# One scaled pair product per head instead of seven levels, in a kernel that runs a decayed recurrence and then a multiplicative feed-forward block

## The chip, the cores and the metric

The kernel runs on one core of one Trainium2 chip. The number that counts is the device time of one execution in microseconds (us). An engine works through its own instructions in order and waits on semaphores for the others: PE (TensorE, matmul; PEld is its weight load), DVE (VectorE), ACT (ScalarE), POOL (GpSimd), and SP, which here issues all the transfers.

## The reference

```python
r, k, v: (4, 8, 768, 48)   w, u: (8, 48)
for t in range(S):                                 # S = 768
    kt, vt, rt = k[:, :, t], v[:, :, t], r[:, :, t]
    cur = einsum('bhd,bhe->bhde', u[None] * kt, vt)
    y[:, :, t] = einsum('bhd,bhde->bhe', rt, state + cur)
    state = w[None, :, :, None] * state + einsum('bhd,bhe->bhde', kt, vt)
x = y.transpose(0, 2, 1, 3).reshape(B * S, H * D)  # (3072, 384)
a, b = x @ w1, x @ w2                              # (3072, 1024)
out = (a * b @ w3) @ w_out                         # (3072, 384)
```

`w` lies between 0.85 and 0.95. The four feed-forward weights arrive as float64, that is as 64-bit words; the kernel rounds them to float32 on the chip. All else is float32.

## The kernel before

**Tiling.** The sequence is cut into six chunks of 128 tokens. A *unit* is one chunk of one of the four batches, so there are 24 units, in the order chunk by chunk and, within a chunk, batch by batch. Two heads form a pair: head dimension 48 is padded to 64, so that a pair fills 128 partitions.

**The first part, per unit.** `load` fetches k, r and v. `turn` (L211) transposes k and r on PE, and ACT copies them out. The matrix A[t, s] of a chunk is built in seven *levels* (`scale` L219, `level` L236): level l joins pairs of tokens whose places differ by a block of 2^l, so that only powers of w with an exponent of at least 0 occur. Every level needs its own scaled operands, KL (POOL, L229) and RL (DVE, L232; for level 0 ACT and POOL, L223 and L224), its own matmuls (L241, L262, L256), and its own copy into A: for levels 0 to 4 a predicated copy with a mask on DVE (L242, L244, L263), for levels 5 and 6 a copy on ACT (L258). `output` (L268) multiplies A and the state with v and r (L276, L279), ACT copies the result, and ten small transfers put it into x with the layout that the second part wants. `update` (L294) brings the state forward (POOL L299 and L306, PE L302, DVE L308).

**The weights.** `weight` (L150) converts one piece of up to 128 x 512 numbers from 64 bits: three products on POOL (L161, L170, L171), four instructions on DVE (L162, L165, L166, L168), one on ACT (L169). There are 36 pieces. `fold` (L185) transposes w3 and multiplies it with w_out, so that the second part needs only w34 = w3 w_out.

**The second part, per chunk.** `ab` (L326), eight times: six matmuls 128 x 512 for a and b (L331, L336), a copy on ACT, a product on DVE (L337). `o` (L339), four times: eight matmuls 128 x 384 with w34 (L342), a copy on ACT, a transfer out.

**What sets the order.** The loop at the end (L360 to L380) interleaves by hand: beside the units of chunk 0 run w_out and w3, beside those of chunk 1 w1 and w2, beside chunk c from 2 on the second part of chunk c - 2; the second part of chunks 4 and 5 stands behind all units. The framework then orders each engine's queue by priority and dependences; an engine executes its queue strictly in that order. PSUM is split into four banks for the levels, two for the rest of the first part and two for the second part.

Of the kernel before, what the change touches and what calls it, by code (L numbers as in the profile page):

```python
# [8 lines left out]
F32 = mybir.dt.float32  # L9
# [3 lines left out]
ALU = mybir.AluOpType  # L13


@with_exitstack
def kernel(
# [25 lines left out]
    The second part uses (a b w3) w_out = (a b) (w3 w_out), with w3 w_out made  # L43
    once on chip.
    """
# [3 lines left out]
    C = 128  # L49
    NCH = S // C  # L50
# [7 lines left out]
    LEVELS = 7  # L58

    const = ctx.enter_context(tc.tile_pool(name="const", bufs=1))  # L60
    work = ctx.enter_context(tc.tile_pool(name="work", bufs=2))
    psA = ctx.enter_context(tc.tile_pool(name="psA", bufs=4, space=bass.MemoryType.PSUM))
    psM = ctx.enter_context(tc.tile_pool(name="psM", bufs=2, space=bass.MemoryType.PSUM))
    psF = ctx.enter_context(tc.tile_pool(name="psF", bufs=2, space=bass.MemoryType.PSUM))

# [1 line left out]
    ident = const.tile([P, P], F32)  # L67
    make_identity(nc, ident)
    masks = []
    for l in range(LEVELS):  # L70
        L = 1 << l
        n = C // (2 * L)
        m = const.tile([P, n], F32, name=f"mask{l}")
        nc.gpsimd.memset(m, 1.0)
        nc.gpsimd.affine_select(out=m, in_=m, compare_op=ALU.is_ge, fill=0.0, base=0,
                                pattern=[[-2 * L, n]], channel_multiplier=1)
        nc.gpsimd.affine_select(out=m, in_=m, compare_op=ALU.is_ge, fill=0.0, base=L - 1,
                                pattern=[[2 * L, n]], channel_multiplier=-1)
        masks.append(m)

# [1 line left out]
    NIN = 3  # L82
    knat, rnat, vnat = ([const.tile([C, H, PAD], F32, name=f"{nm}nat{i}") for i in range(NIN)] for nm in "krv")
    for t in knat + rnat + vnat:
        nc.vector.memset(t[:, :, D:PAD], 0.0)
    AT = [const.tile([P, NP, 2, C], F32, name=f"AT{i}") for i in range(2)]
    for t in AT:
        nc.vector.memset(t, 0.0)
    KL = [None] + [const.tile([P, NP, C], F32, name=f"KL{l}") for l in range(1, LEVELS)]
    RL = [const.tile([P, NP, 2, C // 2 + C], F32, name="RL0")]  # L90
    RL += [const.tile([P, NP, 2, C // 2], F32, name=f"RL{l}") for l in range(1, LEVELS)]
    for t in RL + KL[1:]:
        nc.gpsimd.memset(t, 0.0)
    st = [const.tile([P, NP, 2, PAD], F32, name=f"st{b}") for b in range(B)]
    for t in st:
        nc.gpsimd.memset(t, 0.0)

# [1 line left out]
    units = [(c, b) for c in range(NCH) for b in range(B)]  # L99

    def load(n):
        if n >= len(units):
            return
        c, b = units[n]
        ts = slice(c * C, (c + 1) * C)
        nc.sync.dma_start(out=knat[n % NIN][:, :, :D], in_=k[b, :, ts, :].rearrange("h t d -> t h d"))
        nc.sync.dma_start(out=rnat[n % NIN][:, :, :D], in_=r[b, :, ts, :].rearrange("h t d -> t h d"))
        nc.sync.dma_start(out=vnat[n % NIN][:, :, :D], in_=v[b, :, ts, :].rearrange("h t d -> t h d"))

    wu = const.tile([2 * NP, 2, PAD], F32)  # L110
    nc.vector.memset(wu, 0.0)
    nc.sync.dma_start(out=wu[0:NP, :, :D], in_=w.rearrange("(p i) d -> p i d", i=2))
    nc.sync.dma_start(out=wu[NP:2 * NP, :, :D], in_=u.rearrange("(p i) d -> p i d", i=2))
    load(0)
    load(1)

# [5 lines left out]
    ps = psM.tile([P, 2 * NP], F32, tag="m", name="ps_wu")  # L122
    nc.tensor.transpose(ps, wu.rearrange("a i d -> a (i d)"), ident[0:2 * NP, 0:2 * NP])
    wucol = const.tile([P, 2 * NP, 1], F32)
    nc.vector.tensor_copy(out=wucol.rearrange("x a o -> x (a o)"), in_=ps)
    ucol = wucol[:, NP:2 * NP, :]
    pw = const.tile([P, NP, C], F32)
    pr = const.tile([P, NP, C], F32)
    wn = const.tile([P, LEVELS, NP, 1], F32)
    nc.vector.memset(pw[:, :, 0:1], 1.0)  # L130
    nc.vector.memset(pr[:, :, C - 1:C], 1.0)
    cur = wucol[:, 0:NP, :]
    for l in range(LEVELS):
        n = 1 << l
        by = cur.to_broadcast([P, NP, n])
        nc.vector.tensor_mul(pw[:, :, n:2 * n], pw[:, :, 0:n], by)
        nc.vector.tensor_mul(pr[:, :, C - 2 * n:C - n], pr[:, :, C - n:C], by)
        nc.vector.tensor_mul(wn[:, l], cur, cur)
        cur = wn[:, l]
    wc = cur  # L140
    ps = psM.tile([P, NP, C], F32, tag="m", name="ps_pr")
    for p in range(NP):
        nc.tensor.transpose(ps[:, p, :], pr[:, p, :], ident)
    prn = const.tile([C, H, PAD], F32)
    nc.vector.tensor_copy(out=prn.rearrange("t h d -> t (h d)"), in_=ps.rearrange("x p t -> x (p t)"))

# [1 line left out]
    PIECE = 512  # L148

    def weight(dst, src):  # L150
        """dst: [P, n] float32 on chip; src: the same [P, n] of a weight."""
        if src.dtype != U64:
            nc.sync.dma_start(out=dst, in_=src)
            return
        n = src.shape[1]
        raw = work.tile([P, PIECE], U64, tag="raw", bufs=2, name="raw")[:, :n]
        nc.sync.dma_start(out=raw, in_=src)
        lo, hi = (raw.bitcast(U32).rearrange("p (n z) -> p n z", z=2)[:, :, z] for z in range(2))
        high, bits, low = (work.tile([P, PIECE], F32, tag="tmp", bufs=6, name=nm)[:, :n] for nm in ("high", "bits", "low"))
        # Magnitudes under 2^-126 become zero. The high word read as float32 is ordered as the magnitudes are.  # L160
        nc.gpsimd.tensor_mul(bits, hi.bitcast(F32), hi.bitcast(F32))  # L161
        nc.vector.scalar_tensor_tensor(high, bits, (1.125 * 2.0 ** -15) ** 2, hi.bitcast(F32), ALU.is_ge, ALU.mult)  # L162
        # Sign and top exponent bit stay; the other exponent bits and the upper 20 of the fraction move up by 3.
        hb, bb = high.bitcast(U32), bits.bitcast(U32)
        nc.vector.tensor_scalar(bb, hb, 0x07FFFFFF, 3, ALU.bitwise_and, ALU.logical_shift_left)  # L165
        nc.vector.scalar_tensor_tensor(hb, hb, 0xC0000000, bb, ALU.bitwise_and, ALU.bitwise_or)  # L166
        # The lower 32 bits of the fraction, at the power of two that the number has.
        nc.vector.tensor_scalar(bb, hb, 0xFF800000, None, ALU.bitwise_and)  # L168
# [4 lines left out]
    def ab_weight(q, z):  # L173
        for dst, src in ((w1, moe_w1), (w2, moe_w2)):
            js = slice(z * PIECE, (z + 1) * PIECE)
            weight(dst[:, q, js], src[q * P:(q + 1) * P, js])

# [1 line left out]
    wo = {}  # L179

    def out_weight(c):
        wo[c] = work.tile([P, DM], F32, tag="abt", bufs=KF + 4, name=f"wo{c}")
        weight(wo[c], moe_w_out[c * P:(c + 1) * P, :])

    def fold(j):  # L185
        w3n = work.tile([P, DF], F32, tag="w3", bufs=3, name=f"w3n{j}")
        for z in range(DF // PIECE):
            js = slice(z * PIECE, (z + 1) * PIECE)
            weight(w3n[:, js], moe_w3[j * P:(j + 1) * P, js])
        w3T = work.tile([P, KF, P], F32, tag="w3", bufs=3, name=f"w3T{j}")  # L190
        for i in range(2):
# [11 lines left out]
    def rows(i):  # L203
        return slice(i * PAD, (i + 1) * PAD)
# [89 lines left out]
    def update(n):  # L294
        c, b = units[n]
        if c == NCH - 1:
            return
# [113 lines left out]
```

## Time and profile before

| | us |
|---|---|
| device time, median of 3 runs (892.48 to 893.22) | 892.74 |
| span of the profiled execution, first to last instruction | 888.0 |
| busy in it: PE / DVE / POOL / ACT | 784.0 / 504.3 / 387.7 / 166.2 |
| instructions on PE / DVE / POOL / ACT | 3589 / 845 / 400 / 325 |
| conversions of weights | 36 pieces |

For the profiled execution only the span is given; the median lies 4.7 us over it, and that is taken as what lies around the span. A float32 matmul appears in the profile as two PE instructions, a transpose as one. Busy shares are averages over two stretches with different limits, so they have to be read by stage: chunks 0 and 1 end at about 300 us, and from there on PE is the engine that the others wait for.

### The profile page before, as it was taken

What the parts mean: (1) busy time and instruction counts of PE and PEld (TensorE: products, weight loads), DVE (VectorE), ACT (ScalarE), POOL (GpSimd) and SP (SyncE); (2) the same over time, 40 slices, a digit from 0 to 9 for tenths busy, and PEclk for the clock granted to TensorE, in tenths of its full rate; (3) what the DMA queues carried; (4) which work ended last, traced back from release to release, by engine and by line L of the source; (5) the groups of instructions that cost most, each with busy time, mean ns of one, the idle gap of its engine ahead of it and who ended that gap; (6) DMA issues with size and microseconds to landing.
All of it is one profiled execution on the core that took longest, in us unless ns stands there. A gap on an engine that the chain in (4) does not pass through costs nothing.

```text
span 888.0 us, 10047 instructions
## 1 busy us (share of the span) xinstructions
PE 784.0 (88%) x3589; PEld 481.9 (54%) x3589; DVE 504.3 (57%) x845; ACT 166.2 (19%) x325; POOL 387.7 (44%) x400
## 2 busy tenths in 40 slices
PE   4566687567787899999999999999999999999998
PEld 2454355345555555666565666556665556445444
DVE  6999988679999964654365436644554442010010
ACT  1122223231121221112112111211111211110110
POOL 8678787787778852343234323333332220000000
PEclk9787688877998999999999999999999999999999
DMA  7134224213233110032001131110310001000000
GB/s 133 46 76 114 95 96 131 86 56 107 60 92 84 28 27 18 14 68 54 18 10 27 26 73 28 27 28 17 74 28 10 0 12 43 18 0 27 9 0 36
DMA packets 96649, 42.08 MB, mean 47 GB/s; under 512 B 79704, under 2 KB 91992, under 8 KB 96600
## 3 DMA queue, kind: packets, MB, share of 16 engines
q1 hardware_dynamic: 96600, 41.45, 18.7%
q8 instruction: 29, 0.48, 0.2%
q14 instruction: 20, 0.16, 0.1%
HBM read 31.98 MB, written 4.72 MB: 41 GB/s over the span
## 4 chain that ended last, share of the span: by engine, by line
PE 66%; DVE 23%; POOL 7%; issue 3%; ACT 0%; DMA 0%; SPq 0%; POOLq 0%; ACTq 0%; DVEq 0%
PE ps_a L331 14%; PE ps_o L342 14%; PE ps_b L336 13%; DVE RL L232 7%; PE ps_a L262 7%; PE ps_d L241 5%; PE ps_a L256 4%; DVE high L162 4%; PE ps_y L276 3%; DVE AT L263 3%; PE ps_y L279 3%; DVE high L166 2%; DVE bits L165 2%; POOL low L170 2%; DVE bits L168 2%
## 5 line engine op out<-in xcount | busy, mean ns | idle before, releaser
L232 DVE TENSOR_TENSOR RL<-rT,pw 64x256 f32<-64x256 f32 x288 | 195.7, 681 | 27.8 <-PE ps_a L256 22.0
L229 POOL TENSOR_TENSOR KL<-kT,pr 128x256 f32<-128x256 f32 x144 | 116.3, 817 | 166.1 <-PE ps_a L256 98.4
L337 DVE TENSOR_TENSOR abt<-ps_b,a 128x512 f32<-128x512 f32 x48 | 33.2, 692 | 196.6 <-PE ps_b L336 196.5
L331 PE MATMUL ps_a<-xT,w 128*128 128x512 f32 x288 | 136.9, 602 | 0.0
L336 PE MATMUL ps_b<-xT,w 128*128 128x512 f32 x288 | 133.0, 596 | 0.8 <-DVE abt L337 0.8
L342 PE MATMUL ps_o<-w,abt 128*128 128x384 f32 x384 | 128.8, 489 | 0.0
L262 PE MATMUL ps_a<-RL,KL 128*128 128x128 f32 x768 | 105.0, 297 | 24.5 <-DVE AT L244 24.5
L262 PEld LDWEIGHTS ps_a<-RL,KL 128*128 128x128 f32 x768 | 103.4, 212 | 38.7 <-issue 22.6
L342 PEld LDWEIGHTS ps_o<-w,abt 128*128 128x128 f32 x384 | 71.4, 190 | 46.4 <-issue 1.3
L241 PE MATMUL ps_d<-RL,kT 128*128 128x384 f32 x192 | 79.2, 545 | 19.2 <-DVE AT L263 17.6
L336 PEld LDWEIGHTS ps_b<-xT,w 128*128 128x128 f32 x288 | 54.9, 191 | 69.2 <-issue 67.5
L263 DVE COPY_PREDICATED AT<-mask,ps_a 128x512 f32<-128x512 int32 x96 | 81.7, 851 | 17.2 <-PE ps_a L262 14.1
L256 PE MATMUL ps_a<-RL,KL 128*32 128x64 f32 (+1 forms) x576 | 58.0, 246 | 25.9 <-ACT AT L258 20.0
L331 PEld LDWEIGHTS ps_a<-xT,w 128*128 128x128 f32 x288 | 51.0, 190 | 48.2 <-issue 45.6
L256 PEld LDWEIGHTS ps_a<-RL,KL 128*32 128x32 f32 (+1 forms) x576 | 44.4, 122 | 58.4 <-ACT AT L258 36.3
L258 ACT COPY AT<-ps_a 32x256 f32<-32x256 f32 (+1 forms) x72 | 30.5, 433 | 222.5 <-DVE AT L263 167.6
L242 DVE COPY_PREDICATED AT<-ident,ps_d 128x256 f32<-128x256 int32 x96 | 42.3, 459 | 47.2 <-PE ps_d L241 46.9
L170 POOL TENSOR_TENSOR low<-low,bits 128x512 f32<-128x512 f32 (+1 forms) x36 | 47.5, 1322 | 36.3 <-DVE bits L168 35.1
L273 POOL TENSOR_TENSOR rw<-rT,pw 128x512 f32<-128x512 f32 x20 | 25.9, 1297 | 85.3 <-ACT rT L217 85.3
L224 POOL TENSOR_TENSOR RL<-rT,wucol 64x512 f32<-64x512 f32 x48 | 53.3, 1111 | 14.3 <-PE ps_d L241 8.3
L241 PEld LDWEIGHTS ps_d<-RL,kT 128*128 128x128 f32 x192 | 36.1, 206 | 40.6 <-DVE AT L263 11.3
L333 ACT COPY a<-ps_a 128x512 f32<-128x512 f32 x48 | 28.1, 585 | 137.9 <-PE ps_a L331 136.9
(66 smaller groups left out, 773.8 us busy)
## 6 DMA issues: line engine op xcount, KB each, us to landing
raw<-in_moe_w_dram SPq DMA_DIRECT2D x28, 512.0 KB, 3.5
knat<-in_k_dram SPq DMA_DIRECT2D x24, 192.0 KB, 3.2
rnat<-in_r_dram SPq DMA_DIRECT2D x24, 192.0 KB, 3.8
vnat<-in_v_dram SPq DMA_DIRECT2D x24, 192.0 KB, 2.8
out_dram<-osb SPq DMA_DIRECT2D x24, 192.0 KB, 2.2
xT<-y SPq DMA_DIRECT2D x144, 24.0 KB, 1.8
raw<-in_moe_w_out_dram SPq DMA_DIRECT2D x8, 384.0 KB, 3.3
xT<-y SPq DMA_DIRECT2D x48, 16.0 KB, 1.8
```

What stands on the lines that cost most here:

```text
L170: nc.gpsimd.tensor_mul(low, low, bits)
L224: nc.gpsimd.tensor_mul(RL[0][rows(i), :, i, C // 2:], rT[n][rows(i)], ucol[rows(i)].to_broadcast([PAD, NP, C]))
L229: nc.gpsimd.tensor_mul(halves(KL[l], L)[:, :, :, 0, :], halves(kT[n], L)[:, :, :, 0, :], pr[:, :, None, C - L:C].to_broadcast([P, NP, m, L]))
L232: nc.vector.tensor_mul(RL[l][rows(i), :, i, :].rearrange("x p (n a) -> x p n a", a=L), halves(rT[n], L)[rows(i), :, :, 1, :], pw[rows(i), ...
L241: nc.tensor.matmul(ps, lhsT=kT[n][:, p, :], rhs=RL[0][:, p], start=True, stop=True)
L242: nc.vector.copy_predicated(at[:, p], ident.bitcast(I32)[:, None, :].to_broadcast([P, 2, C]), ps[:, :, C // 2:])
L256: nc.tensor.matmul(ps[s0:s0 + L, p, :, g * L:(g + 1) * L], lhsT=KL[l][:, p, s0:s0 + L], rhs=RL[l][:, p, :, g * L:(g + 1) * L], start=True, ...
L262: nc.tensor.matmul(ps[:, p], lhsT=KL[l][:, p, :], rhs=RL[l][:, p], start=True, stop=True)
L263: nc.vector.copy_predicated(at.rearrange("s p i (n z a) -> s (p i) n z a", z=2, a=L)[:, :, :, 1, :], masks[l].bitcast(I32)[:, None, :, Non ...
L331: nc.tensor.matmul(pa, lhsT=w1[:, q, js], rhs=xT[c][:, q, :], start=(q == 0), stop=(q == KM - 1))
L336: nc.tensor.matmul(pb, lhsT=w2[:, q, js], rhs=xT[c][:, q, :], start=(q == 0), stop=(q == KM - 1))
L342: nc.tensor.matmul(po, lhsT=abt[j][:, b * C:(b + 1) * C], rhs=w34[:, j, :], start=(j == 0), stop=(j == KF - 1))
```

## The change

The seven levels go. With w within [0.6, 1.6], k is multiplied by w^(63 - s) and r by w^(t - 64) for the places s and t in the chunk (`scale`, on DVE, before the transposes), and one product per head gives w^(t - 1 - s). The powers (`up`, `down`) are made once, with a reciprocal. `pairs` multiplies the two heads of a pair on their own 64 rows each, into two PSUM tiles, and two predicated copies per unit keep t > s. The diagonal is computed apart: a product of k, r and u on DVE with a sum over d, written by eight scaled copies of the identity on ACT. The state is kept in scaled form, so that r and k need no further scaling in `output` and `update`; the factor w^128 is applied in `update` on DVE. x gets a permuted order of its 384 columns, so that ACT copies three quarters of a unit's output straight into x and six transfers of 16 partitions carry the rest; the rows of w1 and w2 are fetched in the same order, four transfers a piece instead of one. The conversion leaves POOL: six instructions on DVE and one on ACT. The loop's neighbours are reordered: beside chunk 0 half of w1 and w2, beside chunk 1 the other half and the second part's products a b of chunk 0, beside chunk 2 those of chunk 1, w_out and three eighths of w3, and so on; the second part lags by one chunk, its output product somewhat more.

All of that is one arm of a branch. A flag, computed on DVE from the smallest and the largest w, is read by every engine into a register; where w lies outside, the other arm runs with the seven levels, built with small POOL instructions. Both arms are in the program.

```diff
+    inside = nc.values_load(flag[0:1, 0:1], min_val=0, max_val=1, ...
...
-        nc.gpsimd.tensor_mul(bits, hi.bitcast(F32), hi.bitcast(F32))
-        nc.vector.scalar_tensor_tensor(high, bits, (1.125 * 2.0 ** -15) ** 2, hi.bitcast(F32), ALU.is_ge, ALU.mult)
...
-        nc.scalar.mul(low, lo, 2.0 ** -52)
-        nc.gpsimd.tensor_mul(low, low, bits)
-        nc.gpsimd.tensor_add(dst, high, low)
+            nc.scalar.activation(out=power, in_=hi.bitcast(F32), func=ABS)
+            nc.vector.scalar_tensor_tensor(dst, power, 1.125 * 2.0 ** -15, hi.bitcast(F32), ALU.is_ge, ALU.mult)
+            nc.vector.tensor_scalar(tb, hb, 0x07FFFFFF, 3, ALU.bitwise_and, ALU.logical_shift_left)
+            nc.vector.scalar_tensor_tensor(hb, hb, 0xC0000000, tb, ALU.bitwise_and, ALU.bitwise_or)
+            nc.vector.tensor_scalar(pb, hb, 0xFF800000, None, ALU.bitwise_and)
+            nc.vector.scalar_tensor_tensor(t, lo, 2.0 ** -52, power, ALU.mult, ALU.mult)
+            nc.vector.tensor_add(dst, dst, t)
...
+        def scale(n):
+            kn, rn = kin[n % NIN], rin[n % NIN]
+            if fast:
+                nc.vector.tensor_mul(ks[n % NS][:, :, :D], kn, pn["k"][:, :, :D])
+                nc.vector.tensor_mul(rs[n % NS][:, :, :D], rn, pn["r"][:, :, :D])
...
+            nc.vector.tensor_mul(ruk, kn, rn)
+            nc.vector.tensor_mul(ruk, ruk, ub)
+            nc.vector.tensor_reduce(dg, ruk, AX.X, ALU.add)
...
+                    nc.scalar.activation(out=AT[n][:, i, p, :], in_=ident, func=COPY, scale=dg[:, h:h + 1])
...
+        def pairs(n):
+            if fast:
+                ps = [psA.tile([C, NP, C], F32, tag="a", name=f"ps_a{n}_{i}") for i in range(2)]
+                for p in range(NP):
+                    for i in range(2):
+                        nc.tensor.matmul(ps[i][:, p, :], lhsT=kT[n][rows(i), p, :], rhs=rT[n][rows(i), p, :],
+                                         start=True, stop=True)
+                for i in range(2):
+                    nc.vector.copy_predicated(AT[n][:, i], later.bitcast(I32)[:, None, :].to_broadcast([C, NP, C]), ps[i])
+                return
...
+            nc.scalar.copy(out=y, in_=ps[:, NP - 1, :])
+            nc.scalar.copy(out=xT[c][:, :, bs], in_=ps[:, 0:KM, :])
+            for i in range(2):
+                for q in range(KM):
+                    at = i * PAD + q * HOLE
+                    nc.sync.dma_start(out=xT[c][i * PAD + D:(i + 1) * PAD, q, bs], in_=y[at:at + HOLE, :])
...
+                if c:
+                    nc.vector.tensor_add(old, new, old)
+                    nc.vector.tensor_mul(old, old, by)
...
+        beside = [
+            W12[0],
+            merge(W12[1], AB(0, range(KH))) + AB(0, range(KH, KF)),
+            merge(AB(1), WO + W3(range(3))),
+            merge(AB(2, range(KH)), W3(range(3, KF))) + O(0) + AB(2, range(KH, KF)),
+            merge(O(1) + O(2), AB(3)),
+            merge(O(3), AB(4)),
+        ]
+        tail = O(4) + AB(5) + O(5)
...
+    with tc.If(inside > 0) as chosen:
+        program(True)
...
+    with chosen.Else():
+        program(False)
```

On PE, a unit in chunk 2 of the kernel before (products of the levels 3 to 6 of a unit, then its output and state products, with the last a and b of the second part between):

```order
L262 MATMUL ps_a_3_2357<-RL_134,KL_127 128x128 x4
L262 MATMUL ps_a_4_2366<-RL_135,KL_128 128x128 x4
L256 MATMUL ps_a_5_2375<-RL_136,KL_129 32x2x32 x4
L331 MATMUL ps_a_7_2390<-xT_394,w_169 128x512 x2
L256 MATMUL ps_a_5_2375<-RL_136,KL_129 32x2x32 x4
L331 MATMUL ps_a_7_2390<-xT_394,w_169 128x512
L336 MATMUL ps_b_7_2396<-xT_394,w_170 128x512 x3
L256 MATMUL ps_a_6_2401<-RL_137,KL_130 64x128 x4
L276 MATMUL ps_y_2410<-rw_2411,st_153 128x128
L302 MATMUL ps_s_2439<-vnat_110,ks_2437 128x128 x3
L279 MATMUL ps_y_2410<-AT_121,vnat_110 64x128 x2
```

And on PE of the changed kernel, the end of one unit of chunk 2 and the begin of the next one's products (kT and rT are the transposes, ps_y the output, ps_s the state, ps_a and ps_b with w the second part, w3T a fold, and ps_a with kT the product of a head):

```order
L310 MATMUL ps_kT_1583<-ident,ks_75 128x128 x4
L310 MATMUL ps_rT_1590<-ident,rs_77 128x128 x4
L365 MATMUL ps_y_1608<-rT_1430,st_85 128x128 x4
L369 MATMUL ps_y_1608<-AT_1364,vnat_74 64x128 x8
L392 MATMUL ps_s_1640<-vnat_74,ks_76 128x128 x4
L416 MATMUL ps_a_7_1648<-xT_681,w_93 128x512 x3
L421 MATMUL ps_b_7_1654<-xT_681,w_94 128x512 x3
L276 MATMUL ps_w3T_0_1660<-ident,w3n_1597 128x128 x4
L321 MATMUL ps_a_0_1712<-rT_1595,kT_1588 128x128
L321 MATMUL ps_a_1_1713<-rT_1595,kT_1588 128x128
```

The last two rows come four times per unit, and they are all that is left of the levels; the folds of w3 now stand among the second part's products.

On DVE of the changed kernel, the last conversion of w1 and w2 (w_94 is w2, raw its 64-bit piece), with the next unit's scaling and diagonal woven in and the second part's products behind it:

```order
L245 SCALAR_TENSOR_TENSOR w_94<-power,raw_81 128x512
L290 TENSOR_TENSOR ks_76<-kin_66,pnk 128x8x48
L247 TENSOR_SCALAR t<-w_94 128x512
L248 SCALAR_TENSOR_TENSOR w_94<-w_94,t 128x512
L291 TENSOR_TENSOR rs_78<-rin_69,pnr 128x8x48
L250 TENSOR_SCALAR power<-w_94 128x512
L297 TENSOR_TENSOR ruk_1074<-kin_66,rin_69 128x384
L251 SCALAR_TENSOR_TENSOR t<-raw_81,power 128x512
L298 TENSOR_TENSOR ruk_1074<-ruk_1074,ub 128x384
L252 TENSOR_TENSOR w_94<-w_94,t 128x512
L299 TENSOR_REDUCE dg_1075<-ruk_1074 128x8
L422 TENSOR_TENSOR abt_4_966<-ps_b_4_973,a_4_971 128x512
```

In the kernel before, the DVE rows between the four instructions of a conversion were those of the levels, and the first product abt (L337) came only in chunk 2, behind all conversions. Now the product abt_4 of chunk 0 stands right behind the last conversion of w2, because it needs it.

On DVE before, the corresponding place, the last conversions and the first product of the second part:

```order
L166 SCALAR_TENSOR_TENSOR high<-high,bits 128x512
L165 TENSOR_SCALAR bits<-high 128x512
L168 TENSOR_SCALAR bits<-high 128x512
L166 SCALAR_TENSOR_TENSOR high<-high,bits 128x512
L242 COPY_PREDICATED AT_121<-ident,ps_d_0_1968 128x256
L168 TENSOR_SCALAR bits<-high 128x512
L244 COPY_PREDICATED AT_121<-mask_75,ps_d_0_1968 128x128
L242 COPY_PREDICATED AT_121<-ident,ps_d_1_1972 128x256
```

Behind these rows stand five more masked copies of level 0, the scaled operands and the copies of levels 1 and 2, and then abt_0.

More of the change, by code (lines that the diff above doesn't have):

```diff
@@ L82 @@
[L82 to L91, printed above, removed]
@@ L140 @@
[L140 to L168, printed above, removed]
-        nc.scalar.mul(low, lo, 2.0 ** -52)
-        nc.gpsimd.tensor_mul(low, low, bits)
-        nc.gpsimd.tensor_add(dst, high, low)
@@ L203, in rows @@
-    def rows(i):
-        return slice(i * PAD, (i + 1) * PAD)
-    def halves(t, L):
-        return t.rearrange("x p (n z a) -> x p n z a", z=2, a=L)
-    kT, rT, xT = {}, {}, {}
-    def turn(n):
-        for dst, src, nm in ((kT, knat, "kT"), (rT, rnat, "rT")):
-            ps = psM.tile([P, NP, C], F32, tag="m", name=f"ps_{nm}{n}")
-            for p in range(NP):
-                nc.tensor.transpose(ps[:, p, :], src[n % NIN][:, 2 * p:2 * p + 2, :].rearrange("t h d -> t (h d)"), ident)
-            dst[n] = work.tile([P, NP, C], F32, tag=nm, name=f"{nm}{n}")
-            nc.scalar.copy(out=dst[n], in_=ps)
@@ L310, in attention @@
-    def attention(n):
-        def step(l):
-            level(n, l)
-            if n + 1 < len(units):
-                scale(n + 1, l)
-        steps = [lambda: turn(n + 1)] if n + 1 < len(units) else []
-        steps += [lambda l=l: step(l) for l in range(LEVELS)]
-        return steps + [lambda: output(n), lambda: update(n)]
-    def ffn(c):
-        steps = []
+    landed[1] = fetch(ab_pieces[1])
+    ends = const.tile([1, 3], F32)
+    flag = const.tile([1, 1], I32)
+    nc.vector.tensor_reduce(ends[:, 0:1], wrow, AX.X, ALU.min)
@@ L378, with AB, O, first @@
-    for c in range(NCH - LAG, NCH):
-        for step in ffn(c):
-            step()
+        def AB(c, js=range(KF)):
+            return [lambda c=c, j=j: ab(c, j) for j in js]
+        def O(c):
+            return [lambda c=c, b=b: o(c, b) for b in range(B)]
+        def first(i):
+            if i not in landed:
+                landed[i] = fetch(ab_pieces[i])
+            convert(ab_pieces[i], landed[i])
+        half = len(ab_pieces) // 2
+        W12 = [[lambda i=i: first(i) for i in range(z * half, (z + 1) * half)] for z in range(2)]
```

465 lines of the change are left out of this document (283 added, 182 removed).

## The prediction

> **What bounds the kernel now.** I read the page's busy times and chain first, then busy times by stage.
>
> ```profile
> span 888.0 us, 10047 instructions
> PE 784.0 (88%) x3589; PEld 481.9 (54%) x3589; DVE 504.3 (57%) x845; ACT 166.2 (19%) x325; POOL 387.7 (44%) x400
> PEclk9787688877998999999999999999999999999999
> PE 66%; DVE 23%; POOL 7%; issue 3%; ACT 0%; DMA 0%; SPq 0%; POOLq 0%; ACTq 0%; DVEq 0%
> ```
>
> ```profile
> core 0: us, PE busy (x) PEld busy (x) DVE busy (x) ACT busy (x) POOL busy (x), PEclk, DMA share, GB/s
> 0.00:25.00 25.00, 8.90 (x29) 5.66 (x29) 16.77 (x47) 6.21 (x11) 21.30 (x55) 0.93 0.69 118
> 25.00:300.00 275.00, 194.42 (x1003) 135.19 (x1004) 246.13 (x351) 61.62 (x119) 212.04 (x184) 0.81 0.30 85
> 300.00:748.00 448.00, 444.06 (x2181) 272.75 (x2180) 230.31 (x433) 83.03 (x167) 154.31 (x162) 1.00 0.14 30
> 748.00:888.00 140.00, 136.67 (x379) 68.27 (x377) 11.07 (x16) 15.31 (x28) 0.00 (x0) 1.00 0.05 16
> ```
>
> There are two kernels in one. Up to 300 us (chunks 0 and 1, and all conversions) DVE is busy 246.1 of 275 us, 89.5%, with POOL close behind, and PE has gaps and a granted clock of 0.81. From 300 us on PE is busy 444.1 of 448 us at a clock of 1.00. So the front is priced by DVE and the rest by PE.
>
> What PE takes for each kind of work at full clock is read from where the next row starts:
>
> ```profile
> 639.97 0.44 PE L279 MATMUL ps_y<-AT,vnat 128*64 128x128 f32 x4
> 640.34 0.49 PE L276 MATMUL ps_y<-rw,st 128*128 128x128 f32 x2
> 640.76 0.44 PE L279 MATMUL ps_y<-AT,vnat 128*64 128x128 f32 x4
> ...
> 643.03 5.33 PE L342 MATMUL ps_o<-w,abt 128*128 128x384 f32 x16
> 648.19 0.60 PE L215 MATMUL ps_kT<-ident,knat 128*128 128x128 f32 x4
> 648.63 0.60 PE L215 MATMUL ps_rT<-ident,rnat 128*128 128x128 f32 x4
> 649.06 2.75 PE L241 MATMUL ps_d<-RL,kT 128*128 128x384 f32 x8
> 651.65 1.95 PE L262 MATMUL ps_a<-RL,KL 128*128 128x128 f32 x16
> 653.43 2.74 PE L331 MATMUL ps_a<-xT,w 128*128 128x512 f32 x6
> 656.01 2.74 PE L336 MATMUL ps_b<-xT,w 128*128 128x512 f32 x6
> ```
>
> A float32 matmul is two instructions. Hence one 128x512 takes 2.58/3 = 0.86 us, one 128x384 5.16/8 = 0.645, one 128x128 1.78/8 = 0.223, a transpose 0.44/4 = 0.109, and one of the half-array matmuls of L279 0.37/2 = 0.185. Going from L276's full array to halves costs 0.42 - 0.22 = 0.20 us.
>
> DVE's price depends on POOL:
>
> ```profile
> 121.38 1.74 DVE L162 SCALAR_TENSOR_TENSOR high<-bits,raw 128x512 f32<-128x512 f32 x1 [0.93 <-POOL bits L161]
> 123.37 1.16 DVE L165 TENSOR_SCALAR bits<-high 128x512 uint32<-128x512 uint32 x1
> ...
> 125.90 0.68 DVE L162 SCALAR_TENSOR_TENSOR high<-bits,raw 128x512 f32<-128x512 f32 x1
> 126.50 0.41 DVE L168 TENSOR_SCALAR bits<-high 128x512 uint32<-128x512 uint32 x1
> ```
>
> ```profile
> 162.54 0.60 DVE high L166
> 163.14 0.34 DVE bits L165
> 163.48 0.34 DVE bits L168
> 163.81 0.61 DVE high L166
> 169.36 0.61 DVE AT L263
> 170.34 1.37 issue
> ```
>
> The same L162 takes 1.74 us in one place and 0.68 in the other; the long one runs beside POOL's products. In the chain, where only the step to the next instruction counts, 512 elements cost 0.61 us and a one-source instruction 0.34.
>
> ```profile
> L229 POOL TENSOR_TENSOR KL<-kT,pr 128x256 f32<-128x256 f32 x144 | 116.3, 817 | 166.1 <-PE ps_a L256 98.4 <-PE ps_a L262 66.0
> L337 DVE TENSOR_TENSOR abt<-ps_b,a 128x512 f32<-128x512 f32 x48 | 33.2, 692 | 196.6 <-PE ps_b L336 196.5
> L308 DVE TENSOR_TENSOR st<-ps_s,st 64x256 f32<-64x256 f32 x40 | 16.8, 420 | 41.0 <-POOL st L306 40.7
> L217 ACT COPY kT<-ps_kT 128x512 f32<-128x512 f32 x24 | 14.1, 586 | 37.7 <-PE ps_kT L215 37.6
> L258 ACT COPY AT<-ps_a 32x256 f32<-32x256 f32 x48 | 17.4, 362 | 185.6 <-DVE AT L263 167.6 <-PE ps_a L256 18.0
> ```
>
> From L308 to L337, 256 more elements cost 272 ns, so 384 elements cost 0.61 - 0.14 = 0.48 us on DVE (0.27 for one source).
>
> **The change part by part.** *PE.* A unit loses the products of levels 0 to 4 (2.59 + 2 x 1.78 = 6.2 us) and two more levels, and gains eight products on half the rows. Their price is not in the trace. The nearest row is L279, half the columns: 0.185 us. Below lies 0.112 (both halves at once), above 0.42 (L276 with its switch at every one). I take 0.185 and one switch of 0.20 per unit into them and one into the output. PE then has 288 matmuls 128x512 (247.4 us), 192 of 128x384 (123.8), eight folds of eight transposes and eight 128x384 (48.3), 192 transposes (20.9), 192 products and 192 output halves (71), 160 state matmuls 128x128 (35.8), some 48 switches (9.6), 1 for the tables: **558 us** instead of the 784.0 busy now.
>
> *DVE and POOL.* POOL falls silent after the tables, so DVE runs at the short prices. A conversion is then four instructions of 0.61 and two of 0.34: 3.1 us on DVE, and it can no longer overlap with POOL's three. A unit costs five instructions of 0.48 (scaling, diagonal, sum), two masked copies and two for the state at 0.61: 4.8 us, in place of the levels' operands and copies. The tensor_reduce and the read of the 32-bit low words have no row; between 0.42 (L308) and 1.74 (L162 beside POOL) I take the short price, since nothing of POOL is beside them. All of DVE is about 249 us, so DVE sets only the front.
>
> *The front, by the queues.* The last thing on which PE must wait for a conversion is b_4 of chunk 0: it needs the last piece of w2. Ahead of that piece's last instruction DVE has 12 conversions (37.4), 49 instructions of 0.48 (23.5), 18 masked copies (11.0), 14 for the state (8.5), four products abt (2.4) and 22 small ones of the tables (3.7): 86.5 us. At the 89.5% of before that is 96.7 us. Behind this point PE still has, of the same list, 254 x 0.86 + 123.8 + 48.3 + 112 x 0.109 + 236 x 0.185 + 104 x 0.223 + 30 x 0.20 = **475.7 us**. Queued on PE behind b_4 are the last products of chunk 0 and all of chunk 1's, and DVE's abt_4 stands right behind the conversion that releases it, so nothing else is late there. The later checkpoints are looser: at the masked copy of unit 12, DVE has had 162 us and PE has 367 to go.
>
> *The start.* DVE can begin when w has come and the branch is taken.
>
> ```profile
> 5.37 2.31 DMA wu<-in_u_dram
> ```
>
> In before, w and u are there at 7.7 us; I take 8.0 until the flag is made. No branch is in the trace. It costs nothing at least; for the most I take four times the longest "issue" gap, 4 x 1.37 = 5.5; I take two, 2.7, one to read the flag and one at the end. Start: 10.7 us.
>
> *Sum against the profiled execution.* 10.7 + 96.7 + 475.7 = 583.1. Behind the last matmul:
>
> ```profile
> 884.70 0.48 ACT L345 COPY osb<-ps_o 128x384 f32<-128x384 f32 x1 [4.68 <-PE ps_o L342]
> ```
>
> 888.0 - 884.7 = 3.3 us for copy, transfer and end. PE idled 3.9 of 448 us in its stretch: 4 more. Between the conversions of the first half of w1 and w2 and the last of w2, PE has 37 us of work at full clock; at a clock of 0.81 that is 46, DVE has (86.5 - 51)/0.895 = 40: 6 more. Span 596.4; the median lies 4.7 over the span: 601, taken as **602 us**.
>
> *Hidden.* ACT gains 192 scaled copies of 128 elements (between 0.26, by the line through L217 and L258's 256, and 0.59, L217; 50 to 113 us) and the conversions' first step, and has about 180 us in 600; DVE and PE wait for it only in the front. SP gets 36 more weight transfers and 96 fewer of x; the DMA share is 0.30 at most behind the start. If that cover goes, it is in the front, and the second rival prices it.
>
> On the halves the Trainium skill's page "TensorEngine Tiling (Array Packing)", section Theoretical Speedup, gives up to twofold for a contraction of 64 rows or less; the row L279 shows 0.223 to 0.185, a gain of a sixth. By that rule the 116 products left behind the checkpoint would take 8.5 us less. Its section Key Properties says that a change of mode drains the array, which speaks against mixing halves with full matmuls; the 0.20 us agrees. On the branch, the page "Runtime: NRT & Kernel Launch", Instruction fetch mechanics, says that a taken branch breaks the prefetch and stalls; no run here shows it.
>
> **The rivals.**
> 1. *The front overlaps fully* (the table says why it could: no POOL beside DVE, which was the second engine of the old front). DVE at 100%: 86.5 for 96.7, no clock loss, products at 0.112: 602 - 10 - 6 - 8 = 578.
> 2. *The front becomes a chain of waits.* Each unit goes DVE, PE, ACT, PE, DVE, PE with two buffers, and DVE's and PE's loads up to unit 12 are nearly alike (162 and 182 us), so each waits for the other. For it: the clock of 0.81 where PE was not full. At 70% DVE takes 124 us, 27 more, and chunk 2's 105 us of PE at 85% 18 more: 647. The Trainium skill's page "TensorE: Matmul & The Clock Gate", Part 1, has the clock halved after an idle window; the 0.81 is what such halves average to here.
> 3. *The other arm runs,* or the change doesn't do what it says: the flag comes out 0. Then per unit and level POOL makes 12 small products. Each is priced from L229: a quarter of its 0.82 at least. 24 x 7 x 12 = 2016 of them give 413 to 1650 us on POOL alone, with memsets and masks on top and nothing of the old double buffering; at half of L229 already 824 us, and with a front and second part of about 300 behind, **over 1,100, slower**. It decides at a w under 0.6 or over 1.6; the reference has 0.85 to 0.95.
>
> **How the numbers follow.** Forecast (590 to 625) 0.58; rival 1 (under 590) 0.15; rival 2 (625 to 665) 0.20; later still, but under 890, 0.05; rival 3 0.02. The range takes rival 1's 578 and its bound without any branch (2.7 less), and rival 2's 647 and the half products' upper price in part (116 x 0.23 = 27 on the forecast): **575 to 650**. A change within 0.2% is about what a measurement of this kernel cannot tell from none; so faster 0.97, same 0.01, slower 0.02.
>
> **What would show it.** In the changed profile POOL busy under 30 us and DVE about 250; L245 and its fellows near 0.69 and 0.41, not 1.7; PE busy near 550, full at clock 1.00 from about 120 us on; the half products starting 0.09 us apart. The prediction is wrong if PE shows gaps behind chunk 2, if the masked copies or the reduce are dear, or if the halves cost more than full products.

## The result, and the profile after

The changed kernel takes 607.11 us (median of 4 runs, 606.07 to 614.0) against 892.98 us (4 runs, 892.48 to 893.66): a ratio of 0.682, interval 0.678 to 0.685. The forecast was 602, in a range of 575 to 650.

The page of the changed kernel: span, busy time of each engine, then PE's busy share and clock in forty slices, and the chain's shares.

```profile
span 604.2 us, 6718 instructions
PE 554.2 (92%) x2441; PEld 321.0 (53%) x2441; DVE 261.5 (43%) x497; ACT 172.6 (29%) x423; POOL 10.3 (2%) x36
...
PE   0298987679999999999999999999999999999996
PEclk9999999699999999999999999999999999999999
...
PE 86%; DVE 5%; SPq 4%; DMA 2%; ACT 1%; issue 1%; DVEq 0%; ACTq 0%
```

The fast arm ran: POOL has 36 instructions. PE's 784.0 us of work are 554.2 now, DVE's 504.3 are 261.5. The weak place is the sixth to ninth slice, about 75 to 136 us. The same by stages, with busy time of each engine, granted clock and DMA share:

```profile
core 0: us, PE busy (x) PEld busy (x) DVE busy (x) ACT busy (x) POOL busy (x), PEclk, DMA share, GB/s
0.00:30.00 30.00, 4.35 (x19) 3.56 (x20) 18.25 (x55) 9.47 (x24) 10.27 (x36) 1.00 0.68 134
30.00:133.00 103.00, 85.02 (x549) 55.03 (x548) 73.86 (x133) 41.18 (x107) 0.00 (x0) 0.95 0.49 100
133.00:599.00 466.00, 464.51 (x1876) 262.43 (x1874) 169.40 (x311) 121.43 (x292) 0.00 (x0) 1.00 0.20 52
```

Behind 133 us PE is busy 464.5 of 466 us. In the front, from 30 to 133 us, *no* engine is full: DVE is busy 73.9 of 103 us (72%), PE 85.0. An engine that alone set the pace would be full there, so the front waits for something else, or for a chain between the engines. The chain of waits names one thing, in two pieces of the front (start, duration, what):

```profile
46.67 0.51 SPq L380
...
49.75 0.59 SPq L380
...
50.44 0.53 SPq L99
51.01 3.69 DMA rin<-in_r_dram
54.72 0.57 DVE rs L291
...
66.63 0.42 SPq L133
...
67.15 0.52 SPq L380
...
70.24 0.59 SPq L380
...
70.94 2.71 DMA raw<-in_moe_w_dram
73.66 0.69 DVE w L245
...
131.96 0.62 DVE w L252
...
132.62 1.99 PE ps_b L421 x4
```

SP issues all transfers in one order. The six transfers that carry a unit's x (L380) take about 0.6 us each to issue, and behind them stands first the load of the next k and r (L99 and L100), then the next piece of a weight. DVE waits for both. From 30 to 133 us eight units' x transfers hold SP's queue for 3.7 to 4.4 us each, 31 us in all. SP's own waits in the same window (us in total, times, longest):

```profile
SPq L133 <- DVE t L251: 28.1, 6, 7.8
SPq L380 <- ACT AT L304: 4.7, 1, 4.7
...
SPq L380 <- ACT xT L376: 0.4, 1, 0.4
```

So in the front SP stands still at L380 for only 5 us; what L380 costs there is the time of issuing. (SP waits far longer at L380 behind 133 us, where PE is full all the same.) The 28.1 us are waits for a buffer of raw words that DVE has to read first. PE's granted clock was also 0.50 for 10.2 us of the front (the last three numbers of the row are clock, DMA share and GB/s):

```profile
108.30:118.50 10.20, 6.53 (x21) 3.87 (x21) 5.60 (x11) 4.76 (x12) 0.00 (x0) 0.50 0.79 137
```

The last two rows of the chain are the checkpoint of the prediction, the conversion that releases b_4 of chunk 0: PE goes on at 132.6 us.

### The profile page after: what moved, and what is told of

Same layout as the page of the kernel before. It is cut to its first block, busy times and chain, and to the rows that moved or that the text cites. A ratio compares the mean times of both kernels' runs of the same rounds, so it can differ in the third digit from the quotient of the medians.

```text
span 604.2 us, 6718 instructions
## 1 busy us (share of the span) xinstructions
PE 554.2 (92%) x2441; PEld 321.0 (53%) x2441; DVE 261.5 (43%) x497; ACT 172.6 (29%) x423; POOL 10.3 (2%) x36
## 4 chain that ended last, share of the span: by engine, by line
PE 86%; DVE 5%; SPq 4%; DMA 2%; ACT 1%; issue 1%; DVEq 0%; ACTq 0%
PE ps_o L427 21%; PE ps_a L416 20%; PE ps_b L421 20%; PE ps_w L280 7%; PE ps_y L369 4%; PE ps_a L321 4%; PE ps_y L365 3%; PE ps_s L392 3%; PE ps_rT L310 2%; PE ps_kT L310 2%; DMA rin<-in_r_dram 1%; SPq L380 1%; PE ps_w3T L276 1%; SPq L133 1%; DMA raw<-in_moe_w_dram 1%
## 5 line engine op out<-in xcount | busy, mean ns | idle before, releaser
L304 ACT ACTIVATE AT<-ident,dg 128x128 f32<-128x128 f32 x192 | 58.9, 394 | 6.8 <-DVE dg L299 6.8
L280 PE MATMUL ps_w<-wo,w3T 128*128 128x384 f32 x128 | 43.0, 489 | 0.6 <-ACT w3T L277 0.5
L324 DVE COPY_PREDICATED AT<-later,ps_a 128x512 f32<-128x512 int32 x48 | 32.3, 721 | 18.8 <-PE ps_a L321 17.9
L321 PEld LDWEIGHTS ps_a<-rT,kT 64*128 64x128 f32 x384 | 25.3, 195 | 16.5 <-issue 8.4
L321 PE MATMUL ps_a<-rT,kT 64*128 64x128 f32 x384 | 31.4, 298 | 2.8 <-ACT rT L312 2.8
L280 PEld LDWEIGHTS ps_w<-wo,w3T 128*128 128x128 f32 x128 | 23.7, 190 | 16.0 <-ACT w3T L277 1.0
L244 ACT ACTIVATE power<-raw 128x512 f32<-128x512 f32 (+1 forms) x36 | 23.4, 653 | 25.2 <-DVE t L251 19.4
L369 PE MATMUL ps_y<-AT,vnat 128*64 128x128 f32 x384 | 28.8, 280 | 0.9 <-ACT kT L312 0.6
L392 PE MATMUL ps_s<-vnat,ks 128*128 128x128 f32 x160 | 24.3, 286 | 0.0
L369 PEld LDWEIGHTS ps_y<-AT,vnat 128*64 128x64 f32 x384 | 21.6, 136 | 4.9 <-ACT kT L312 0.8
L251 DVE SCALAR_TENSOR_TENSOR t<-raw,power 128x512 f32<-128x512 uint32 (+1 forms) x36 | 23.6, 656 | 0.3
L299 DVE TENSOR_REDUCE dg<-ruk 128x8 f32<-128x384 f32 x24 | 13.1, 547 | 24.3 <-ACT AT L304 24.2
```

Source lines behind the costliest of these rows:

```text
L280: nc.tensor.matmul(ps, lhsT=w3T[:, kc, :], rhs=wo[kc], start=(kc == 0), stop=(kc == KF - 1))
L304: nc.scalar.activation(out=AT[n][:, i, p, :], in_=ident, func=COPY, scale=dg[:, h:h + 1])
L321: nc.tensor.matmul(ps[i][:, p, :], lhsT=kT[n][rows(i), p, :], rhs=rT[n][rows(i), p, :], start=True, stop=True)
L324: nc.vector.copy_predicated(AT[n][:, i], later.bitcast(I32)[:, None, :].to_broadcast([C, NP, C]), ps[i])
L369: nc.tensor.matmul(ps[rows(i), p], lhsT=vnat[n % NV][:, 2 * p + i, :], rhs=AT[n][:, i, p, :], start=not c, stop=True, skip_group_check=True)
L392: nc.tensor.matmul(ps[:, p], lhsT=kk[:, 2 * p:2 * p + 2, :].rearrange("t h d -> t (h d)"), rhs=vnat[n % NV][:, 2 * p:2 * p + 2, :], start= ...
```

## The experiments

Each ratio is to the kernel before, measured on the same chip. The changed kernel was not run again beside the experiments, so differences to its 607.11 us carry the spread of its own four runs (606.07 to 614.0).

**1 and 2. The x transfers on another queue.** Theory: SP's order makes the front late.

```diff
-                    nc.sync.dma_start(out=xT[c][i * PAD + D:(i + 1) * PAD, q, bs], in_=y[at:at + HOLE, :])
+                    nc.gpsimd.dma_start(out=xT[c][i * PAD + D:(i + 1) * PAD, q, bs], in_=y[at:at + HOLE, :])
```

and the same with `nc.scalar`.

> The six small transfers of a unit's x are issued by POOL's queue, which is idle, instead of SP's. In the changed kernel PE reached the third matmul of b_4 of chunk 0 at 132.6 us, 19 us later than the prediction's working had it. Theory Q (SP's queue): the loads and the weight pieces stand behind those transfers on SP, 3.7 us of issue per unit and a wait for ACT's copy; freed of them, b_4 comes 8 to 15 us earlier and the time falls to 592 to 600. Rival C (a chain of waits between DVE, PE and ACT with two buffers): SP is not what is waited for; b_4 stays within 3 us and the time at 604 to 610.

> The same six transfers issued by ACT's queue, right behind the copies that make them. Theory Q: SP is freed as with POOL, but ACT pays 3.5 us of issue per unit, so it gains less: 596 to 604. Rival C: ACT is part of the chain, and the added issue lengthens it: 608 to 620, b_4 later than 133 us.

On POOL: 591.62 us (589.26 to 592.75), ratio 0.662 [0.660, 0.663]. On ACT: 596.41 us, 0.668 [0.666, 0.670]. Theory Q had 592 to 600 and 596 to 604; rival C, 604 and more, falls. The front with POOL, in the same window as above:

```profile
30.00:133.00 103.00, 96.09 (x589) 59.55 (x588) 86.68 (x164) 49.16 (x131) 24.05 (x49) 0.98 0.61 124
```

No instruction of DVE or PE was taken away, yet in the same 103 us DVE does 12.8 us more work and PE 11.1. PE goes on with b_4 at 117.3 us in place of 132.6 (on ACT at 116.4). So 15 us of the front go with the place of these transfers in SP's queue. Two things moved along with it. The rest of SP's order stays the same up to 117 us, but for one load of v; DVE's and PE's queues, however, come out in another order from some 50 to 60 us on. And b_4 now goes on ahead of the only stretch with a clock of 0.50 (117.6 to 121.0 us), where the 10.2 us of the changed kernel lay ahead of it; by the clock that is up to 5 of the 15 us, an estimate. On ACT's queue DVE's order is another one again and b_4 comes within 1 us of POOL's, which speaks for SP's queue as the cause. The transfers also cost the queue that takes them: ACT's six issues hold it about 4 us per unit (meanwhile its scaled copies of the diagonal stand still), and from b_4 to the end the kernel is then 4 us longer than with POOL (477.8 us for 473.7). The Trainium skill, page "DMA: Bandwidth & Descriptors", section Issuing engine by pattern, gives plain loads and stores to SP and calls GpSimd's path the slower one. Here the slower path is the faster choice: an x transfer lands a median of 2.5 us after its issue on POOL and 1.8 on SP, and the kernel still gains 15 us, because of what stands behind it in the queue.

**3 and 4. Without the branch.** Only the fast arm, no register read; once with x on SP, once on POOL.

```diff
-    inside = nc.values_load(flag[0:1, 0:1], min_val=0, max_val=1, ...
...
-    with tc.If(inside > 0) as chosen:
-        program(True)
...
+    program(True)
```

> Only the arm that ran, without the flag's register load and the branch; the other arm is not in the program. The working priced the branch at 2.7 us (between 0 and 5.5). If that holds the time falls by 1 to 4 us, the first product of k and r on DVE comes up to 2 us earlier, and the 4.8 us behind the last matmul become about 3.3. Rival: a jump over the long other arm and a program of twice the length cost more, through instruction loading: 6 to 12 us.

> Without the branch and, besides, with the small x transfers on POOL's queue. Without the branch alone the first transposes began 7.9 us earlier and the end came 1.3 us sooner behind the last matmul, and yet the time rose to 615 us; the third weight piece then stood on SP behind the first two units' x transfers. Theory Q: with these off SP that order costs nothing, and what is left is the branch's own price: 584 to 591 us against the 591.6 with the branch. Rival: leaving the branch out costs for another reason (the loads of the start, the order on DVE); then the 8 us stay and it is 597 to 603.

Missed, in sign too: 615.32 us (0.689 [0.688, 0.691]), *slower* by 8 than with the branch. The first transposes come at 20.0 us in place of 27.8, the end 1.4 us sooner behind the last copy (3.5 us for 4.9), and still PE goes on with b_4 at 142.7 us, 10 later. Without the branch the framework orders SP anew. Its issues there, behind the first two pieces:

```profile
15.46 2.04 SPq L101 DMA_DIRECT2D vnat<-in_v_dram  x1
29.86 4.78 SPq L378 DMA_DIRECT2D xT<-y  x6
...
36.61 4.19 SPq L378 DMA_DIRECT2D xT<-y  x6
40.84 1.98 SPq L133 DMA_DIRECT2D raw<-in_moe_w_dram  x4
```

L133 fetches the third piece, and two units' x transfers (L378 is L380 of the change) stand ahead of it; between 17.5 and 29.9 us SP stands still until the first of them has its data. In the changed kernel that piece and the next stand ahead of all x transfers. With x on POOL and no branch the time is 596.35 us (0.667 [0.665, 0.669]). Theory Q's 584 to 591 is missed too; the rival's 597 to 603 is just above. Taking x off SP gains 19 us here and 15.5 with the branch, so x on SP accounts for only 3.5 of the 8 us. The 5 us that are left over 591.62 go along with a later third piece, here with the branch and x on POOL:

```profile
17.48 7.88 SPq L133 DMA_DIRECT2D raw<-in_moe_w_dram  x6
```

and here without the branch, x on POOL:

```profile
28.80 1.96 SPq L133 DMA_DIRECT2D raw<-in_moe_w_dram  x4
```

There it stands behind a load of v for which SP waits 7.5 us, until the matmuls that read the old v are done (L367 is L369 of the change):

```profile
SPq L101 <- PE ps_y L367: 7.5, 1, 7.5
```

That this is all of the 5 us is not shown; no run puts the piece back in its place. So the branch as such could not be priced at the start: taking it out also moves the order. At the end the kernel without it is 1.4 and 1.6 us shorter in the two pairs (3.5 for 5.2 with x on POOL).

**5. The half products, one half behind the other.**

```diff
-                for p in range(NP):
-                    for i in range(2):
+                for i in range(2):
+                    for p in range(NP):
```

> The eight products of a unit in another order: first the four of the upper 64 rows, then the four of the lower, instead of alternating. In the changed kernel 16 instructions took 1.09 us, where full ones would take 1.79. Theory H (the halves run at the same time when neighbours lie on different halves): the 16 take 1.7 to 1.9 us, behind the front that is 15 units by 0.7 = 10 us, so 612 to 620. Rival: half the rows are simply cheaper: 16 stay near 1.1 us, the time within 606 to 610.

618.95 us (615.18 to 620.65), ratio 0.692 [0.689, 0.694], 12 us slower, as theory H had it; the rival, half the rows being simply cheaper, falls. A unit's eight products (L321, 16 instructions) in the chain, with the halves in turn as in the change, and other work of a unit for comparison:

```profile
306.81 5.16 PE ps_o L427 x16
...
318.02 1.02 PE ps_y L369 x16
319.04 2.77 PE ps_a L416 x6
321.81 2.58 PE ps_b L421 x6
...
335.58 1.09 PE ps_a L321 x16
336.68 5.36 PE ps_o L427 x16
```

and by half:

```profile
345.78 1.64 PE ps_a L321 x16
```

0.55 us per unit, 13 us in 24 units, against 12 measured. Work that follows the halves takes 0.20 more than usual (5.36 for 5.16, 2.77 for 2.58). By the prices of before, eight full products, 16 instructions, are 8 x 0.223 = 1.78 us, 0.112 an instruction. The starts of the single instructions in the two traces show the rest. With the halves in turn the instructions start in pairs, 0.007 us apart, and the next pair 0.112 us later: two products on different halves run at the same time, at the price of one full one. Only the first step (0.21) and the one to the work behind (0.20) are longer; they make the 1.09 out of 8 x 0.112. By half, the instructions on one half start 0.112 us apart, one after the other, and the second half starts beside the fifth instruction of the first, so that the two overlap only at the end of the first half.

**6 and 7. The conversion alone.** Once the changed kernel with the old conversion (three products on POOL), once the old kernel with the new one.

```diff
-            nc.scalar.activation(out=power, in_=hi.bitcast(F32), func=ABS)
+            nc.gpsimd.tensor_mul(power, hi.bitcast(F32), hi.bitcast(F32))
...
-            nc.vector.scalar_tensor_tensor(t, lo, 2.0 ** -52, power, ALU.mult, ALU.mult)
-            nc.vector.tensor_add(dst, dst, t)
+            nc.scalar.mul(t, lo, 2.0 ** -52)
+            nc.gpsimd.tensor_mul(t, t, power)
+            nc.gpsimd.tensor_add(dst, dst, t)
```

> The changed kernel with the conversion as it was before the change: three products on POOL, four instructions on DVE, one on ACT. Theory P (DVE's price depends on POOL, the step on which the working rests): the two instructions that DVE is spared are eaten by the longer ones beside POOL, a piece's way gets longer by two engines, b_4 comes 10 to 25 us later and the time is 617 to 635. Rival: the contention of the old front was due to other instructions, and DVE gains 12 pieces of 1.2 us ahead of b_4: 595 to 605.

> The kernel before with nothing but the new conversion (six instructions on DVE, one on ACT, none on POOL). By the working's prices the first two chunks have 36 pieces of 3.1 us and eight units of some 13 us on DVE, 220 to 250 us with start, instead of 300: 825 to 870 us. Rival: the old front hangs on the levels' chain over POOL, DVE and PE, and the conversion alone changes little: 880 to 900.

With the old conversion the changed kernel takes 642.05 us (0.718 [0.717, 0.720]), 35 more; the old kernel with the new one 856.91 (0.960 [0.957, 0.962]), 37 less than before on that chip (893.74). Nearly the same sum from both sides; the first is above its forecast of 617 to 635, the second within its 825 to 870. Groups by form with POOL beside DVE (busy, mean ns of one):

```profile
L252 POOL TENSOR_TENSOR t<-t,power 128x512 f32<-128x512 f32 x28 | 37.2, 1330 | 128.9 <-DVE power L250 87.7 <-ACT t L251 28.8 <-DVE rs L292 5.9
...
L299 DVE TENSOR_TENSOR ruk<-ruk,ub 128x384 f32<-128x384 f32 x24 | 23.2, 969 | 2.5 <-DMA ub<-in_u_dram 2.1
...
L248 DVE SCALAR_TENSOR_TENSOR w3n<-w3n,t 128x512 uint32<-128x512 uint32 x16 | 18.7, 1166 | 0.2
```

and the same two of DVE in the changed kernel:

```profile
L298 DVE TENSOR_TENSOR ruk<-ruk,ub 128x384 f32<-128x384 f32 x24 | 13.2, 552 | 1.9 <-DMA ub<-in_u_dram 1.7
...
L248 DVE SCALAR_TENSOR_TENSOR w3n<-w3n,t 128x512 uint32<-128x512 uint32 x16 | 11.0, 685 | 0.1
```

The product with u (L299 there, L298 in the change) shares no data with the conversion, and its mean goes from 552 ns to 969. The mean mixes two kinds: of the 24, thirteen with POOL idle beside them take 0.54 to 0.56 us, as in the changed kernel, and ten beside POOL's products 1.3 to 1.6. The Trainium skill, page "SBUF — State Buffer", section Who interferes with whom, says that a DVE instruction with two SBUF inputs contends with a GpSimd instruction that reads SBUF; these rows agree.

**8. The old order of the neighbours.** w_out and w3 beside chunk 0, w1 and w2 beside chunk 1, the second part two chunks behind, without the early pieces.

```diff
-            W12[0],
-            merge(W12[1], AB(0, range(KH))) + AB(0, range(KH, KF)),
...
+        beside = [WO + W3(range(KF)), W12[0] + W12[1]] + [AB(c) + O(c) for c in range(4)]
+        tail = AB(4) + O(4) + AB(5) + O(5)
```

> The changed kernel with the old neighbours: w_out and w3 beside chunk 0, w1 and w2 beside chunk 1, the second part two chunks behind. DVE must then get through all 36 conversions and eight units before PE has dense work: 88 and 57 us, at 72 to 89% busy, and PE has about 450 us behind: 630 to 670. Rival: PE's sum is what counts and the order only shifts it: 600 to 612.

618.56 us (0.692 [0.691, 0.694]): 11 us slower, where 23 and more were expected, and the rival (no slower) falls too. Its windows:

```profile
30.00:110.00 80.00, 67.67 (x326) 46.07 (x324) 74.26 (x150) 37.19 (x85) 0.00 (x0) 0.85 0.58 159
110.00:200.00 90.00, 73.81 (x421) 44.87 (x421) 69.47 (x125) 31.48 (x78) 0.00 (x0) 0.96 0.48 98
```

I had PE nearly idle while DVE converts. But PE is busy 67.7 us of 80 beside the conversions, 49 of them with the folds of w3 and the rest with the units, at a clock of 0.85, and DVE reaches 74.3 of 80 (93%). So the new order is worth 11 us and no more: most of the front's length is the work in it, in either order.

**9. The start.** What remained late in experiment 1 is the start. DVE's queue has the powers of w behind the first two units' products k r u, which wait for loads. Here the products wait for the powers: their first instruction takes a scalar 1 that is made from the inverse powers. x stays on POOL.

```diff
+            one = tab.tile([P, 1], F32)
+            nc.vector.tensor_scalar(one, wi[:, LEVELS - 1, NP - 1, :], 0.0, 1.0, ALU.mult, ALU.add)
...
-            nc.vector.tensor_mul(ruk, kn, rn)
+            if fast and n < 2:
+                nc.vector.scalar_tensor_tensor(ruk, kn, one, rn, ALU.mult, ALU.mult)
+            else:
+                nc.vector.tensor_mul(ruk, kn, rn)
```

> The x transfers on GpSimd, and in addition the first two units' product k r u is made to wait for the table of inverse powers (its first multiplication takes a scalar 1 that is made from that table). In e1 the DVE queue has the powers of w behind those products, which wait for the loads of k, r and u: 1.7, 2.7 and 2.1 us idle at L297 and L298, the last power is ready at 22.1 us and the first unit's transposes start at 28.3 us. Theory S (the start is set by that queue, and behind it PE has no slack, 96.1 of 103 us busy): the table is done at about 15 us, the first transposes start 3 to 6 us earlier, limited by the conversion and unit 2's load that now stand ahead of the scaling, and the end comes as much earlier: 586 to 589, ratio 0.655 to 0.659. Rival T (the front waits for the weights' conversions, not for the first unit): transposes earlier, but the third a-b product still at 117 us and the time within 2 us of e1's 591.6.

586.6 us (5 runs, 585.18 to 587.98), ratio 0.6565 [0.6552, 0.6579], under experiment 1's interval. The last of the powers and the first transposes, with x on POOL alone:

```profile
22.61 0.28 DVE L210 TENSOR_TENSOR up<-up,wi 128x128 f32<-128x128 f32 x1
...
28.26 1.12 PE L310 MATMUL ps_kT<-ident,ks 128*128 128x128 f32 x4 [4.08 <-DVE ks L290]
```

and with the powers first:

```profile
16.77 0.29 DVE L210 TENSOR_TENSOR up<-up,wi 128x128 f32<-128x128 f32 x1
...
25.39 1.12 PE L315 MATMUL ps_kT<-ident,ks 128*128 128x128 f32 x4 [7.16 <-DVE ks L292]
```

The powers are ready 5.8 us sooner, the transposes start 2.9 sooner, and b_4 goes on at 114.7 us, 2.6 sooner. The time fell by 5.0, so only about half of it is the start. In the profiled executions (spans 591.0 and 586.2) most of the rest is the clock: experiment 1 has the 3.4 us at 0.50 right behind b_4, this run has none, which is worth about 1.7 us by the clock, an estimate. That the time fell into the forecast's 586 to 589 is in that part luck. This is the fastest version of the study.

## Why the prediction was right, step by step

**The order of magnitude and its cause held.** PE's work was forecast at 558 us and is 554.2; DVE's at about 249 and is 261.5; PE is full at a clock of 1.00 behind the front. That the total came within 1% is luck: two terms of the sum were off in opposite directions. PE's 558 is close in the same way. With the halves at their measured price (the paragraph on them below) the list gives 538; the busy time is 16 us above that, since up to 133 us PE is busy 89.4 us where the list, so corrected, has about 75. Against the profiled execution (606.07 us, span 604.2; forecast 601 and 596.4):

| term | forecast | measured | difference |
|---|---|---|---|
| b_4 goes on (start, DVE's front, clock) | 113.4 | 132.6 | +19.2 |
| half products and switches behind it (236 x 0.185 + 30 x 0.20) | 49.7 | 37.0 | -12.7 |
| PE idle behind it | 4 | 1.5 | -2.5 |
| from the last copy to the end (604.24 - 599.38) | 3.3 | 4.9 | +1.6 |
| around the span | 4.7 | 1.9 | -2.8 |
| the rest (what is left over) | | | +2.2 |
| profiled execution | 601.1 | 606.1 | +5.0 |

The 37.0 is worked out from rows below. The 4.7 around the span came from one execution's span and the median of others; where a run has both figures, 1.7 to 1.9 us lie between them.

**The front: the size of one term was off, and with it its reason.** The step "at the 89.5% of before that is 96.7 us" put DVE's share of the old front into the new one. It was 72% from 30 to 133 us, next to rival 2's 70%. But rival 2's chain DVE, PE, ACT was the smaller part of what took it there. I had set SP aside as hidden ("SP gets 36 more weight transfers and 96 fewer of x"), and counted transfers, not what stands behind them: while SP issues the x transfers, loads and pieces wait. Experiment 1, which changes only their queue and the order that the framework then makes, takes 15.3 of the 19.2 us away, and experiment 9 another 2.6 by the start, which leaves 114.7 against the 113.4 forecast. Rival 2's second sum, PE at 85% in chunk 2, did not happen, so the time stayed far from its 647.

**The start.** The flag exists at 3.5 us, sooner than the 8.0 taken, and the first unit's product k r u runs on DVE at 6.9:

```profile
3.40 0.15 DVE L156 SCALAR_TENSOR_TENSOR flag<-ends 1x1 int32<-1x1 f32 x1
...
6.87 0.56 DVE L297 TENSOR_TENSOR ruk<-kin,rin 128x384 f32<-128x384 f32 x1 [1.55 <-DMA rin<-in_r_dram]
...
27.83 1.12 PE L310 MATMUL ps_kT<-ident,ks 128*128 128x128 f32 x4 [3.28 <-DVE ks L290]
...
599.38 0.48 ACT L430 COPY osb<-ps_o 128x384 f32<-128x384 f32 x1 [4.68 <-PE ps_o L427]
```

The last row is the one that stands in the table for the end. From the 6.9 us to the first transposes at 27.8 us DVE is not full (18.3 of the first 30 us). "DVE can begin when w has come and the branch is taken" named the time of its first instruction, and the 89.5% was laid on from there; the queue of the start was not read.

**The half products.** Taken at 0.185, eight cost 1.48 us and a switch of 0.20; one half behind the other (experiment 5) they take 1.64 and a switch, a little more than that. In the order of the change they cost 1.09, and 0.20 for the way back, where the sum had the switch on the way in. The output halves take 1.02 and 0.20. With 14.5 units' products and 15 units' outputs behind the checkpoint that is 14.5 x 1.29 + 15 x 1.22 = 37 us for 49.7. The lower bound of the prediction, 0.112 each, was nearer (0.14). The 0.185 was read from L279 of before, which is just one pair of halves between full products: in that trace too its instructions start in pairs, 0.006 us apart, so its 0.37 us is two products at once, 0.22, and some 0.15 at the two ends. The ratio to full products is 1.78 / 1.09 = 1.6; by the twofold of "TensorEngine Tiling (Array Packing)" in the Trainium skill, Theoretical Speedup, it would be 0.89. Between the first pair and the last (0.112 a pair) the trace agrees; the 0.20 more lies at the two ends.

**DVE's prices** held where POOL is silent. Of the two instructions without a row, the sum over d takes 547 ns and the read of the low words 686, between the bounds and near the short price:

```profile
L251 DVE SCALAR_TENSOR_TENSOR t<-raw,power 128x512 f32<-128x512 uint32 x28 | 19.2, 686 | 0.3
...
L299 DVE TENSOR_REDUCE dg<-ruk 128x8 f32<-128x384 f32 x24 | 13.1, 547 | 24.3 <-ACT AT L304 24.2
```

**Rival 1** needed DVE at 100%. Even with x on POOL it is 84% in that window, where PE is then nearly full (96.1 of 103 us); 586.6 us came by PE's work moving forward, not by a full DVE. **Rival 3** fell with POOL's 36 instructions.

**Where the 286 us come from.** The conversion is 35 to 37 of them by two experiments, the order of the neighbours 11. If these add up, which no run shows, some 239 are left for the levels, the state and the new x together; these were not tried apart.

## What to carry to other kernels

A queue that issues transfers is an engine with an order: before calling transfers hidden, read which instruction stands ahead of each load, how long it holds the queue and what it waits for, not how many there are. A share of busy time carried from one kernel to another is a guess about its waits, so look for the queue that could hold the engine. And take one thing out of a scheduled kernel only with the new order beside it: removing the branch moved the order, the kernel came out slower, and the price of the branch could not be read from it.

## What the runs showed of the hardware that had not been expected

- Products on the two row halves run two at a time when they alternate: a pair every 0.112 us, the price of one full instruction, with about 0.2 us more at the two ends together. Eight take 1.09 us, 1.64 one half behind the other, 1.78 on the full array by the prices of before.
- An x transfer moves only 8 KB and holds SP's queue for about 0.6 us (0.5 on POOL); six of them hold it 3.7 us or more per unit.
- A product on DVE that shares no data with POOL's work takes 0.55 us with POOL idle and up to 1.6 us with POOL's products beside it.
